# What releases the loads of two granules: landed q transposes of the granule ahead, in place of x transposes two granules before

## The chip, the cores and the metric

The kernel runs on one core of one Trainium2 chip. The metric is the device time of one execution in microseconds (us). Before the change three runs took 208.42, 208.58 and 208.96 us; the median is 208.58 us.

## The reference

The reference is a windowed attention followed by a two-layer feed-forward block. Cut to what matters:

```python
# q, k, v: (4, 8, 768, 64): batch, heads, positions, head size
scores = (q @ k.T) / sqrt(64)
keep = (first 8 keys) | (0 <= i - j < 96)         # global keys and a local window
scores = where(keep, scores - slope[h] * dist, -1e9)
a = softmax(scores)
x = (a @ v), heads side by side                    # (3072, 512)
out = (s * relu(x @ w_in) ** 2 + b) @ w_out        # w_in 512 x 2048, w_out 2048 x 512
```

Inputs and output are float32; the kernel computes in bf16 with sums in float32.

## The kernel before, in words

The 3072 tokens are cut into 12 granules of 256 positions (`NJ`), three for each of the four batches; a granule is two blocks of 128. Each granule goes through the same stations:

- Loads. `load_granule` (lines 110 to 117) issues six DMAs from GpSimd: k and q of the first block, k and q of the second (into the tile `nat`, one of four buffers, `j % 4`), and v of the two blocks (into `vb`). They read float32 from HBM and write bf16; each brings 128 KB. They stand in the trace at lines 116 and 108 (for granules that are loaded piece by piece, at 102 and 108).
- Transposes of k and q. Granules 0 to 3 are transposed on TensorE. From granule 4 on `qk_by_dma` (lines 356 to 363) issues four DMA transposes from SyncE (k, q of the first block, k, q of the second), from `nat` into the tiles `kx` and `qx`. Each is 128 x 512 bf16.
- Scores and attention. `stage_S` (`scores`) multiplies on TensorE at line 441, ScalarE takes the exponential (line 450), VectorE multiplies by a template of the mask (line 457). `stage_A` multiplies by v at line 495, VectorE normalizes into `xn` (lines 465 and 466).
- Transposes of x. `finish_granule` (lines 950 to 957) turns `xn` into `xT`, on TensorE for granules 0 to 3, by two DMA transposes from SyncE (line 599) from granule 4 on.
- The feed-forward block. Its first product is at line 619 (`ps<-xT,w_in_bf`), its second at lines 667 and 819. The stores of the output go out from SyncE at lines 687, 704, 848 and 850.

The order of the work is written out by hand: each engine runs its instructions in program order, and there is no scheduler behind it. The opening (lines 1010 to 1143) is a list of calls; from line 1150 on `step(s, ...)` (lines 959 to 989) does half a granule a time: granule `j = 2 * s // 4`. A step asks for the transposes of granule `j + 2` (if it is the first step of a granule from 4 on), issues the scores of step `s + 1`, then does its two units of attention with pieces of the feed-forward block between them; the second step of a granule calls `finish_granule`, and, for some granules, copies shifted v (`load_voff`, lines 307 to 319, from SyncE). So the scores of granule 5 begin in step 9, of granule 6 in step 11, of granule 7 in step 13, of granule 8 in step 15.

What lets loads start is `hold_loads` (lines 120 to 122): GpSimd copies one element of a tile, and so waits until that tile is written; all loads behind it in GpSimd's queue wait with it. In the kernel before, `finish_granule(j)` puts such a gate on `xT` of granule `j` and, behind it, the loads of granule `j + 4` (`LEAD`), for `j` from 2 to 7. So the loads of granules 6 and 7 are behind the x transposes of granules 2 and 3, which TensorE makes. The loads of granules 4 and 5 are issued before, at lines 1078 to 1082, without a gate. Granule 6's transposes are asked for in step 8 and granule 7's in step 10, both from SyncE, whose queue also carries the stores, the x transposes and the copies of shifted v, in program order.

Of the kernel before, what the change touches and what calls it, by code (L numbers as in the profile page):

```python
# [17 lines left out]
def kernel(  # L18
# [14 lines left out]
    P = nc.NUM_PARTITIONS  # L33
# [9 lines left out]
    HP = H // 2  # L43
    KC = DM // P
    FC = DF // P
    NJ = B * NGR
# [22 lines left out]
    LEAD = 4  # L69
# [5 lines left out]
    NB = S // P  # L75
# [6 lines left out]
    def nat_tile(j):  # L82
        if j not in nat:
            nat[j] = ldp.tile([P, 2, GB, H, D], BF16, name="nat", tag=f"nat{j % 4}", bufs=1)
        return nat[j]
# [3 lines left out]
    def rows_of(src, b, sb):  # L89
        return src[b, :, sb * P : (sb + 1) * P, :].rearrange("h p d -> p h d")  # L90
# [13 lines left out]
    def load_v(j, blocks=range(GB)):  # L104
        b, g = divmod(j, NGR)
        for i in blocks:
            sb = g * GB + i
            nc.gpsimd.dma_start(vbuf[b % 2][:, sb, :, 0:D], rows_of(v, b, sb))  # L108

    def load_granule(j):  # L110
        b, g = divmod(j, NGR)
        t = nat_tile(j)
        for i in range(GB):
            sb = g * GB + i
            for n in range(2):
                nc.gpsimd.dma_start(t[:, n, i, :, :], rows_of(srcs[n], b, sb))  # L116
        load_v(j)


    def hold_loads(ap):  # L120
        g = work.tile([P, 1], BF16, name="gate", tag="gate")
        nc.gpsimd.tensor_copy(g[0:1, :], ap)  # L122
# [156 lines left out]
    def qk_of(b, n):  # L279

        if b not in qk:
            qk[b] = (
                qkp.tile([P, NB, HP, P + (NG + 15) // 16 * 16], BF16, name="kx", tag="kx"),
                qkp.tile([P, NB, HP, P], BF16, name="qx", tag="qx"),
            )
        return qk[b][n][:, :, :, 0:P]
# [9 lines left out]
    def attach(b, lo, hi):  # L296

        kx = qk[b][0]
        nc.vector.tensor_copy(
            kx[:, lo:hi, :, P : P + NG],  # L300
            kx[:, 0, :, 0:NG].unsqueeze(1).to_broadcast((P, hi - lo, HP, NG)),
        )
# [53 lines left out]
    def qk_by_dma(j):  # L356
        b, g = divmod(j, NGR)
        for i in range(GB):
            for n in range(2):
                nc.sync.dma_start_transpose(  # L360
                    qk_of(b, n)[:, g * GB + i],
                    nat[j][:, n, i, :, :].rearrange("p h d -> p (h d)"),
                )
# [12 lines left out]
    def make_koff(j, blocks=range(GB)):  # L376
        b, g = divmod(j, NGR)
        if g == 0 or j >= SHIFT:
            return
        kx, ko = qk[b][0], koff_of(j)  # L380
        i0, n = blocks[0], len(blocks)
        lo = g * GB - 1 + i0
        nc.vector.tensor_copy(ko[:, i0 : i0 + n], kx[:, lo : lo + n, :, 0:P])
        nc.vector.tensor_copy(
            ko[:, i0 : i0 + n, :, 0:NG],
            kx[:, 0, :, 0:NG].unsqueeze(1).to_broadcast((P, n, HP, NG)),
        )
# [83 lines left out]
    def stage_A(u, pool=None):  # L471
        j, hp, b, g = unit(u)
        first = g == 0
        pt = st.pop(u)
        vn = vbuf[b % 2]
        if pool is None:
            av = ps_av.tile([P, GB, 2, VW], F32, name="ps_av", tag="av")
        else:
            av = pool.tile([P, GB, 2, VW], F32, name="ps_av2", tag="psh")
        if j not in xn:  # L480
            xn[j] = xpool.tile([P, GB, DM], BF16, name="xn", tag="xn")
        if first:
            dcol, ocol = ((0, 1), (None, 2)) if j < BIAS_PE else ((1, 2), (None, 0))
        else:
            dcol, ocol = (0, 3), (1, 2)
        for i in range(GB):
            for hi in range(2):
                h = 2 * hp + hi
                terms = [(dcol[i], vn[:, g * GB + i, h, 0 : D + 1])]
                if not first:  # L490
                    terms.append((ocol[i], voff_of(j)[:, i, h, 0 : D + 1]))
                elif i == 1:
                    terms.append((ocol[i], vn[:, 0, h, 0 : D + 1]))
                for n, (c, vv) in enumerate(terms):
                    nc.tensor.matmul(  # L495
                        av[:, i, hi, 0 : D + 1],
                        lhsT=pt[:, hi, c * P : (c + 1) * P],
                        rhs=vv,
                        start=(n == 0),
                        stop=(n == len(terms) - 1),  # L500
                    )
        normalize(
            xn[j][:, :, 2 * hp * D : (2 * hp + 2) * D].rearrange("p i (h d) -> p i h d", d=D), av
        )
# [78 lines left out]
    def x_by_pe(j, evac=(nc.vector.tensor_copy, nc.scalar.copy)):  # L583
        t = xT_tile(j)
        nk = KC // len(evac)
        for e, ev in enumerate(evac):
            ps = ps_h.tile([P, nk, GT], BF16, name="ps_x", tag="psh")
            for kc in range(nk):
                for i in range(GB):
                    c = (e * nk + kc) * P  # L590
                    nc.tensor.transpose(
                        ps[:, kc, i * P : (i + 1) * P], xn[j][:, i, c : c + P], ident_bf[:]
                    )
            ev(t[:, e * nk : (e + 1) * nk, :], ps[:])  # L594

    def x_by_dma(j):
        t = xT_tile(j)
        for i in range(GB):
            nc.sync.dma_start_transpose(t[:, :, i * P : (i + 1) * P], xn[j][:, i, :])

    def g_of(j):

        if j // 2 not in gT:
            gT[j // 2] = gpool.tile([P, FC, 2 * GT], BF16, name="gT", tag="gT")
        return gT[j // 2][:, :, (j % 2) * GT : (j % 2 + 1) * GT]
# [6 lines left out]
    def p1_mm(j, fp):  # L612

        g = g_of(j)
        ps = ps_h.tile([P, 2, GT], F32, name="ps_1", tag="psh")
        for i in range(2):
            fc = 2 * fp + i
            for kc in range(KC):
                nc.tensor.matmul(  # L619
                    ps[:, i, :],  # L620
                    lhsT=w_in_bf[:, kc, fc * P : (fc + 1) * P],
                    rhs=xT[j][:, kc, :],
                    start=(kc == 0),
                    stop=(kc == KC - 1),
                )
        gs = g[:, 2 * fp : 2 * fp + 2, :]

        def relu():
            nc.scalar.activation(gs, ps[:], ACT.Relu)  # L629

        def square():
            nc.vector.tensor_tensor(gs, gs, gs, ALU.mult)  # L632

        return relu, square
# [77 lines left out]
    def flush():  # L712
        while outs:
            outs.pop(0)()
# [222 lines left out]
    def run(cs):  # L937
        for c in cs:
            c()

    def scores(s):
        if s >= NU // 2:
            return []
        _, mms, posts = zip(*[stage_S(u) for u in (2 * s, 2 * s + 1)])
        for part in range(2):
            for mm in mms:
                mm(part)
        return posts[0] + posts[1]

    def finish_granule(j):  # L950
        if j < X_PE:
            x_by_pe(j)
        else:
            x_by_dma(j)
        if 6 <= j + LEAD < NJ:
            hold_loads(xT[j][0:1, 0, GT - 1 : GT])
            load_granule(j + LEAD)

    def step(s, c0, c1, c2, pool=None, pre=()):

        j = 2 * s // HP
        last = (2 * s + 2) % HP == 0
        if not last and j >= 4 and j + 2 < NJ:
            qk_by_dma(j + 2)
        posts = scores(s + 1)
        exps, masks = [c for i, c in enumerate(posts) if i % 2 == 0], posts[1::2]
        run(exps)
        run(pre)
        run(masks)
        run(c0)  # L970
        stage_A(2 * s)
        flush()
        if not last and j + 1 == QK_PE + 1:
            make_koff(j + 1)
        if not last and j % NGR == 0:
            attach(j // NGR, 1, NB)
        run(c1)
        stage_A(2 * s + 1, pool)
        flush()
        n = 2 if j < X_PE else 1  # L980
        run(c2[0:n])
        if last:
            finish_granule(j)
            if SHIFT < j + 2 < NJ:
                load_voff(j + 2)
        run(c2[n:])
        flush()
        if not last and j < SHIFT:
            make_voff(j + 1)
# [130 lines left out]
    p2_mm(1, 1, FC // 2 + 3, FC)  # L1120
    p2_hold(1, 1)
    finish_granule(2)
    s6 = scores(6)
    run(s6)
# [4 lines left out]
    run(scores(7))  # L1129
    run(p1[2][3:5])  # L1130
    qk_by_dma(5)
    r0, q0 = p1_mm(2, 5)
    r0()
    stage_A(14)
# [2 lines left out]
    make_koff(4)  # L1137
    run(p1[2][6:8])
    finish_granule(3)
    run(scores(8))  # L1140
    make_voff(4)
# [110 lines left out]
```

The softmax here doesn't subtract the row's maximum and nothing guards it: scores larger than these inputs give would overflow.

## Time and profile before

| | before |
|---|---|
| median of three runs | 208.58 us |
| lowest and highest run | 208.42 and 208.96 us |
| the profiled execution | 209.15 us |
| its span, first to last instruction | 207.4 us |
| mean granted TensorE clock | 0.998 |
| TensorE busy | 202.1 us |
| VectorE busy | 161.3 us |
| ScalarE busy | 128.5 us |
| GpSimd busy | 68.9 us |
| DMA packets and bytes | 110,836 and 28.17 MB |

The profile is of one execution. Times in it count from the start of its span. PE is TensorE, PEld its weight loads, DVE VectorE, ACT ScalarE, POOL GpSimd and SP SyncE; POOLq and SPq are the queues from which these two issue DMAs. A row of a timeline gives the start, the length, the engine, the line, the operation with the tile that is written and the tile that is read, the number of instructions put together in the row, and, in square brackets, how long the engine had been idle and what ended that. A row of the waits gives who waited, for whom, the total in us, the number of times and the longest. The chain of waits is followed back from the last instruction: at each step to what released it. A DMA's row on its queue is the time in which it is issued; when its data have landed is told apart from that.

### The profile page before, as it was taken

The page shows a single profiled execution, that of the slowest core. Times are in us where ns is not written, and L with a number is a line of the kernel's source. Part 1 is how long each engine was busy: PE and PEld are TensorE (multiplying, and loading weights), DVE is VectorE, ACT ScalarE, POOL GpSimd, SP SyncE. Part 2 cuts the span into 40 slices and gives each one's busy share as a digit, 9 for nine tenths or more (in the row PEclk, how much of TensorE's full clock was granted, in tenths as well). Part 3 has the DMA queues.
Part 4 walks back from the last instruction along what each step waited for, and adds up shares of the span by engine and source line. Part 5 has one row for each costly group of instructions (what it writes and reads, how often), then busy time and mean ns, then how long its engine had stood idle before and what let it go on. Part 6 is the DMA issues. An engine that isn't in the chain of part 4 may idle for free.

```text
span 207.4 us, 5323 instructions
## 1 busy us (share of the span) xinstructions
PE 202.1 (97%) x2191; PEld 160.1 (77%) x2191; DVE 161.3 (78%) x338; ACT 128.5 (62%) x198; POOL 68.9 (33%) x90
## 2 busy tenths in 40 slices
PE   7999999999999999999999999999999999999993
PEld 2678884557867485878888898888888889888883
DVE  7786599977989856799799974699866696737974
ACT  5875669486976548786664595663695764476200
POOL 8985333799365300810900828200000000000000
PEclk9999999999999999999999999999999999999999
DMA  5999999999999999999999999999570300240006
GB/s 164 172 179 202 207 206 177 155 152 129 110 150 120 151 132 218 155 213 212 152 198 153 125 154 178 194 172 126 52 206 0 95 14 0 56 150 0 0 9 196
DMA packets 110836, 28.17 MB, mean 136 GB/s; under 512 B 97852, under 2 KB 109308, under 8 KB 110812
## 3 DMA queue, kind: packets, MB, share of 16 engines
q0 software_dynamic: 76000, 13.11, 90.1%
q1 hardware_dynamic: 33612, 14.13, 41.7%
q10 hardware_dynamic: 1200, 0.59, 1.1%
q8 instruction: 17, 0.28, 0.6%
q14 instruction: 7, 0.06, 0.1%
HBM read 27.26 MB, written 6.29 MB: 162 GB/s over the span
## 4 chain that ended last, share of the span: by engine, by line
PE 65%; DMA 23%; POOL 9%; issue 1%; DVE 0%; POOLq 0%
PE ps L619 29%; PE ps L819 24%; DMA nat<-in_q_dram 12%; DMA w_in_bf<-in_moe_w_in_dram 6%; PE ps L667 5%; DMA qx<-nat 4%; PE ps_s L441 4%; PE ps_av L495 3%; POOL vb L108 3%; POOL nat L102 3%; POOL w_in_bf L140 2%; POOL nat L116 1%; PE ps_last L819 0%; DVE o_last L828 0%; POOL rel L173 0%
## 5 line engine op out<-in xcount | busy, mean ns | idle before, releaser
L619 PE MATMUL ps<-xT,w_in_bf 128*128 128x256 bf16 x768 | 90.3, 273 | 0.0
L629 ACT ACTIVATE gT<-ps 128x512 bf16<-128x512 f32 x96 | 55.8, 599 | 46.8 <-PE ps L619 46.6
L619 PEld LDWEIGHTS <-w_in_bf 128*128 128x128 bf16 x768 | 73.0, 98 | 9.4 <-DVE xT L594 0.2
L450 ACT ACTIVATE pt<-ps_s 128x1024 bf16<-128x1024 f32 (+1 forms) x44 | 39.3, 946 | 3.3 <-PE ps_s L441 3.3
L667 PE MATMUL ps<-w_out_bf,gT 128*128 128x512 bf16 x128 | 29.7, 380 | 0.0
L457 DVE TENSOR_TENSOR pt<-pt,tmpl 128x1024 bf16<-128x1024 bf16 (+1 forms) x40 | 24.6, 645 | 3.8 <-ACT pt L450 3.7
L819 PEld LDWEIGHTS <-gsum 128*128 128x128 bf16 x256 | 24.1, 98 | 3.7 <-DVE gsum L782 0.5
L108 POOL DMA_DIRECT2D vb<-in_v_dram x24 | 21.4, 906 | 6.9 <-DMA w_out_bf<-in_moe_w_out_dram 3.4
L793 DVE TENSOR_TENSOR gT<-gT 128x1024 bf16<-128x1024 bf16 x20 | 13.7, 686 | 11.7 <-ACT gT L629 11.7
L667 PEld LDWEIGHTS <-gT 128*128 128x128 bf16 x128 | 11.7, 98 | 13.0
L466 DVE TENSOR_TENSOR xn<-ps_av,rc 128x256 bf16<-128x256 f32 x48 | 20.4, 425 | 1.7
L819 PEld LDWEIGHTS <-gT 128*128 128x128 bf16 x200 | 18.6, 98 | 2.3
L465 DVE RECIPROCAL rc<-ps_av 128x4 f32<-128x4 f32 x48 | 8.6, 179 | 12.3 <-PE ps_av L495 10.4
L116 POOL DMA_DIRECT2D nat<-in_k_dram x16 | 14.2, 885 | 9.2 <-DMA nat<-in_k_dram 5.1
L495 PEld LDWEIGHTS <-pt 128*128 128x128 bf16 x320 | 14.4, 97 | 2.7 <-DVE xn L466 0.7
L632 DVE TENSOR_TENSOR gT<-gT 128x512 bf16<-128x512 bf16 x32 | 13.0, 422 | 3.5 <-ACT gT L629 3.3
L495 PE MATMUL ps_av<-vb,pt 128*128 128x65 bf16 x208 | 15.5, 193 | 0.0
L819 PE MATMUL ps<-w_out_bf,gsum 128*128 128x256 bf16 x128 | 15.3, 273 | 0.0
L116 POOL DMA_DIRECT2D nat<-in_q_dram x16 | 14.2, 888 | 2.9 <-DMA w_in_bf<-in_moe_w_in_dram 1.9
L819 PE MATMUL ps<-wsub,gsum 128*128 128x256 bf16 x128 | 15.1, 273 | 0.0
L819 PE MATMUL ps<-w_out_bf,gT 128*128 128x256 bf16 x120 | 13.9, 273 | 0.0
L122 POOL COPY gate<-xT 1x1 bf16<-1x1 bf16 x6 | 1.1, 176 | 35.9 <-DMA xT<-xn 35.9
(112 smaller groups left out, 228.5 us busy)
## 6 DMA issues: line engine op xcount, KB each, us to landing
out_dram<-o_q SPq DMA_DIRECT2D x15, 256.0 KB, 2.6
vb<-in_v_dram POOLq DMA_DIRECT2D x24, 128.0 KB, 8.3
nat<-in_k_dram POOLq DMA_DIRECT2D x22, 128.0 KB, 7.7
nat<-in_q_dram POOLq DMA_DIRECT2D x22, 128.0 KB, 7.6
w_out_bf<-in_moe_w_out_dram POOLq DMA_DIRECT2D x4, 512.0 KB, 16.2
w_in_bf<-in_moe_w_in_dram POOLq DMA_DIRECT2D x4, 256.0 KB, 7.4
w_in_bf<-in_moe_w_in_dram POOLq DMA_DIRECT2D x2, 512.0 KB, 11.3
out_dram<-o_sb SPq DMA_DIRECT2D x4, 256.0 KB, 6.3
```

The source lines that it names most:

```text
L108: nc.gpsimd.dma_start(vbuf[b % 2][:, sb, :, 0:D], rows_of(v, b, sb))
L116: nc.gpsimd.dma_start(t[:, n, i, :, :], rows_of(srcs[n], b, sb))
L450: nc.scalar.activation(pt[:, :, 0:ncol], ps[:, :, 0:ncol], ACT.Exp, scale=QSCALE)
L457: nc.vector.tensor_tensor(pv, pv, m.rearrange("p h a c -> p h (a c)"), ALU.mult)
L466: nc.vector.tensor_tensor(dst, av[:, :, :, 0:D], rc[:].to_broadcast((P, 2, 2, D)), ALU.mult)
L495: nc.tensor.matmul(av[:, i, hi, 0 : D + 1], lhsT=pt[:, hi, c * P : (c + 1) * P], rhs=vv, start=(n == 0), stop=(n == len(terms) - 1),)
L619: nc.tensor.matmul(ps[:, i, :], lhsT=w_in_bf[:, kc, fc * P : (fc + 1) * P], rhs=xT[j][:, kc, :], start=(kc == 0), stop=(kc == KC - 1),)
L629: nc.scalar.activation(gs, ps[:], ACT.Relu)
L632: nc.vector.tensor_tensor(gs, gs, gs, ALU.mult)
L667: nc.tensor.matmul(po[:], lhsT=g_of(j)[:, fc, tb * P : (tb + 1) * P], rhs=w_out_bf[:, fc, :], start=(fc == 0), stop=(fc == FC - 1),)
L793: outs.append(lambda: nc.vector.tensor_tensor(gs, gs, gs, ALU.mult))
L819: nc.tensor.matmul(ps[:, tb, cs], lhsT=stat[:, fc, tb * P : (tb + 1) * P], rhs=mov[:, fc, cs], start=(fc == 0), stop=(fc == NH - 1),)
```

## The change

The gate in `finish_granule` now serves only granules from 8 on (`j` from 4). The loads of granule 6 get a gate of their own in the opening: they stand behind the call that issues the transposes of granule 5, and wait until the last of these four (q of the second block) has landed. The loads of granule 7 likewise stand behind the transposes of granule 6 in step 8, and wait for the last of those. The same loads, the same transposes and the same number of gate copies are issued, each engine's instructions keep their order, and nothing else in the program differs.

```diff
 def finish_granule(j):
     if j < X_PE:
         x_by_pe(j)
     else:
         x_by_dma(j)
-    if 6 <= j + LEAD < NJ:
+    if 8 <= j + LEAD < NJ:
         hold_loads(xT[j][0:1, 0, GT - 1 : GT])
         load_granule(j + LEAD)
...
 def step(s, c0, c1, c2, pool=None, pre=()):
...
         if not last and j >= 4 and j + 2 < NJ:
             qk_by_dma(j + 2)
+            if j == 4:
+                hold_loads(qk_of(2, 1)[0:1, 1, HP - 1, P - 1 : P])
+                load_granule(7)
...
     run(p1[2][3:5])
     qk_by_dma(5)
+    hold_loads(qk_of(1, 1)[0:1, NB - 1, HP - 1, P - 1 : P])
+    load_granule(6)
     r0, q0 = p1_mm(2, 5)
```

## The prediction

> **What bounds the kernel now.** I read the page's busy shares first, then what TensorE waited for, then the chain that ended last around those waits, then the queues of GpSimd and SyncE in order of time. The page says that TensorE is the bound:
>
> ```profile
> PE 202.1 (97%) x2191; PEld 160.1 (77%) x2191; DVE 161.3 (78%) x338; ACT 128.5 (62%) x198; POOL 68.9 (33%) x90
> ```
>
> TensorE works 202.1 of 207.4 us. No change of DMA order can give back more than its idle time, so the list of its waits is the ceiling of any gain:
>
> ```profile
> PE ps_w L161 <- DVE idle L151: 1.2, 1, 1.2
> PE ps_s L441 <- DMA qx<-nat: 0.5, 1, 0.5
> ```
>
> The first stands at the start, before any load of this change. Only the second, once, 0.5 us, can be touched. The chain of waits shows how it comes about (start, length, what):
>
> ```profile
> 48.56 11.61 DMA nat<-in_q_dram
> 60.17 0.02 issue
> 60.19 8.86 DMA qx<-nat
> 69.06 0.04 issue
> 69.10 0.57 PE ps_s L441 x14
> ```
>
> The last q block of granule 5 takes 11.61 us to load, its transpose by DMA another 8.86, and TensorE takes up the scores of granule 5 (in step 9) at 69.10. From there the chain runs on TensorE to the end, so the wait is on the path, and a later one would be as well. The GpSimd queue shows what ran beside that transpose (start, us, line, what, idle before):
>
> ```profile
> 51.16 0.18 POOL L122 COPY gate<-xT 1x1 bf16<-1x1 bf16 x1
> 51.28 0.88 POOL L116 DMA_DIRECT2D nat<-in_k_dram  x1
> ...
> 61.62 0.18 POOL L122 COPY gate<-xT 1x1 bf16<-1x1 bf16 x1
> 61.74 0.87 POOL L116 DMA_DIRECT2D nat<-in_k_dram  x1
> ...
> 83.29 0.18 POOL L122 COPY gate<-xT 1x1 bf16<-1x1 bf16 x1 [11.86 <-DMA xT<-xn]
> ```
>
> The 12 loads of granules 6 and 7 are issued between 51.28 and 71.4 us and occupy the DMA engines to about 80 us. The question is when each is needed. In TensorE's timeline the scores are entered at 68.4 (granule 5; 0.5 us of waiting follows), 81.7 (granule 6), 94.1 (granule 7) and 108.7 (granule 8).
>
> [...]in the DMA view of 65.5 to 66 us
>
> ```profile
> q0 software_dynamic: 207, 0.03, 80.0%
> q1 hardware_dynamic: 204, 0.05, 78.9%
> ```
>
> GpSimd's loads (q0) and SyncE's transposes (q1) share one to one, some 410 packets a us each; 1,194 packets a us of q0 alone went between 59.2 and 60.2 us, and 1,102 of q1 alone between 82.6 and 83.6. A load is 1,024 packets, a transpose 512, so a transpose takes some 1.25 us beside loads and 0.5 us alone. [...]all these loads stay in one queue in program order; the trace shows all 68 k, q and v loads there. [...]here a load with nothing else queued still took 4.1 us to land (granule 10's first).
>
> **The change, part by part.**
>
> 1. Removed: two gates (0.18 us each on GpSimd) on the x transposes of granules 2 and 3. Added: two like them, on the last q transposes of granules 5 and 6. GpSimd is idle between its loads, and behind a waiting gate stand only later loads. Cost of the copies themselves: nothing. SyncE's own order does not change, only the time at which its transposes find their data.
>
> 2. Loads of granule 6 leave the stretch from 51 us. Queue q0 is in order, so granule 5's k, q and v loads, already ahead, land when they do now (60.17 for the last q, about 61.5 for v). After that q0 is empty, and granule 5's transposes have the engines alone: four of them at 0.5 us, the last issued at 60.19 to 61.73. The lightly loaded transposes of granule 9 landed 2.5 and 3.4 us after issue; with a remainder of v in the way I take 4.1: landed at 64.3 (bounds 63 and 66) instead of 69.06. TensorE wants it at 68.4, so the 0.5 us stall goes: **-0.5 us**, and all needs below move up by 0.5.
>
> 3. Each later granule now goes through a link "gate, 4 k/q loads, 4 transposes". Its price stands in the trace: granule 10's gate opens at 114.52, its first load is issued at 115.12, SyncE issues the last transpose at 124.05 to 125.27 and that lands at 127.77 (read from the landing events). So gate to the end of issue on SyncE is 10.75 us and gate to landed 13.25. Upper bound: granule 8's loads took 10.3 us from gate to the last q landing (83.29 to 93.6), and the page's median landing of a loaded transpose is near 6, so 16.5 us. Lower: 12.
>  - Granule 6: gate 64.3, landed 77.5, needed at 81.2: slack 3.7 us.
>  - Granule 7: gate 77.5, landed 90.8, needed at 93.6: slack 2.8 us. Two links in series, so an error of 1 us in each takes 2 of it.
>
> 4. What stands behind these transposes on SyncE. Its queue is in order, so x transposes and stores wait for granule 6's and 7's loads too. After granule 6's four (issued until 64.3 + 10.75 = 75.05) come two stores at some 0.53, then the x transposes of granule 4: free at 76.1. Today they start at 76.17 because their data (DVE's xn) end at 76.13. No cost. After granule 7's four (until 77.5 + 10.75 = 88.3) come one store and three early stores, four at about 0.5, then the x transposes of granule 5: about 90.3, where today it is
>
> ```profile
> 84.49 0.53 SPq L687 DMA_DIRECT2D out_dram<-o_sb  x1
> 85.11 4.64 SPq L704 DMA_DIRECT2D out_dram<-o_early  x3
> 89.92 2.96 SPq L599 DMA_TRANSPOSE xT<-xn  x2
> ```
>
>  These landed at 97.6 (the gate of granule 9 opens at 97.71), and TensorE uses them at 98.35: 0.65 us of slack is all there is. With 0.4 us lost on SyncE, the need 0.5 us earlier, and 1 MB of stores now issued in 2 us ahead of them rather than spread over 5, I take 0.9 to 1 us less slack: a new wait of **+0.3 us** at the first phase-1 matmuls of granule 5 (step 13). Bounds: 0 if the stores drain as before; 2 if both links come out 1 us longer.
>
> 5. Loads of granule 8: their gate (x of granule 4) should still open by 83, but GpSimd is issuing granule 7's loads until 77.5 + 0.6 + 5.3 = 83.4. So they start at about 84, as now (83.87). Granule 7's v, last in its group of loads, lands near 89; the copies that read it (`load_voff`, on SyncE at 93) don't wait. From granule 8 on the order is that of today; the scores of granule 8 are needed at 108.2 and its transposes start on SyncE near 95.9 against 95.59 today. Nothing.
>
> Sum: -0.5 + 0.3 = -0.2 us. The profiled execution took 209.15 us (span 207.4, some 1.75 around it) and gives 208.95; the median of the runs shown is 208.58, 0.57 below that, so I forecast 208.58 - 0.2 = **208.4 us**.
>
> **Rivals.**
>
> - *Clean gain.* The x transposes of granule 5 land in time as well, and the whole 0.5 us stays: 208.1. For it: stores may drain faster with q0 briefly empty; against: 0.65 us of slack today is little. More than 0.5 is not there to be had.
> - *The series of links is too long (the other side).* Mechanism: the loads of granules 6 and 7 can no longer run ahead; each link must end before the next begins, and SyncE, blocked in front of granule 7's transposes, holds back the x transposes of granule 5. It decides from a link of about 13.6 us upward (slack gone on x of granule 5) and 14.6 (scores of granule 7, whose slack is 2.8 over two links). At 15 us a link, SyncE is done with granule 7 at 64.3 + 15 + 12.5 = 91.8, the x transposes start near 93.8, 3.9 after today's: stall 3.9 - 0.65 + 0.5 = 3.7 if all of it shows, some 2 if the later, lighter queue q0 gives part back. Net +1.5: 210.1. For it: the medians in loaded stretches (7.4 us for a load, 6 to 7 for a transpose); against: granule 10's link, a like one, took 13.25. At the upper 16.5 the time would reach some 212.
> - *The transposes of granule 5 don't land earlier.* If what delays them isn't q0's share, the stall stays and the chain begins at 69.1: granule 6 landed at 82.3, granule 7 at 95.6, x of granule 5 later by 5: some 211. Against it: the one-to-one sharing above.
>
> **How the numbers follow.** A measurement of this kernel can tell about 0.3%, 0.63 us, from no change. Forecast (a part given back) 0.45, within that bound; clean gain 0.2, of which 0.06 is read as faster by over 0.3% through scatter; links too long 0.3, slower; no earlier transposes 0.05, slower. Of the forecast's chance, 0.02 goes to slower. So faster 0.06, same 0.57, slower 0.37. The range runs from the clean gain less the scatter of the runs (0.2) to the 15 us link: 207.9 to 210.1; above it lies about 0.17. The cases of the likely sign alone have 207.9 to 208.9.
>
> **What would show it.** The wait of L441 on qx at 69 us gone and the landing of that transpose near 64 (step 2); the gates of granules 6 and 7 at about 64.3 and 77.5 (step 3); the scores of granules 6 and 7 without a wait; the x transposes of granule 5 issued near 90.3 and a short TensorE wait for them at 98 (step 4); granule 8's loads from 84 (step 5). I am wrong if a link takes over 14 us, if TensorE waits at the scores of granule 7, or if the first gate opens after 66.

## The result, and the profile after

| | before | after |
|---|---|---|
| median of four runs | 208.50 us | 214.16 us |
| lowest and highest run | 208.34 and 208.96 | 212.82 and 214.91 |
| ratio, 95% interval | | 1.026 (1.0206 to 1.0315) |
| the profiled execution | 209.15 us | 213.95 us |
| its span | 207.4 us | 212.2 us |
| TensorE busy | 202.1 us | 203.5 us |
| mean granted clock | 0.998 | 0.991 |

The change makes the kernel 2.6% slower; the forecast was 208.4 us, no measurable difference, with a range that ended at 210.1. Here and below a ratio leaves out executions more than 1.5% above the fastest of the same kernel, while a median keeps them.

TensorE's longest waits in the changed kernel (who waited for whom, total, times, longest):

```profile
PE ps L619 <- DMA xT<-xn: 3.0, 1, 3.0
PE ps_w L161 <- DVE idle L151: 1.2, 1, 1.2
PE ps_s L441 <- ACT qx L331: 0.3, 1, 0.3
PE ps_s L441 <- DMA qx<-nat: 0.2, 1, 0.2
```

The first row is new: 3 us on x of a granule. The wait of before (L441 on qx at 69 us) is gone; the L441 row on qx that is here now stands elsewhere, as TensorE's timeline shows:

```profile
93.75 0.23 PE L441 MATMUL ps_s<-qx,kx 64*128 64x128 bf16 x2
94.23 0.57 PE L441 MATMUL ps_s<-qx,kx 64*128 64x128 bf16 x14 [0.24 <-DMA qx<-nat]
94.73 3.67 PE L819 MATMUL ps<-w_out_bf,gT 128*128 128x256 bf16 x32
98.23 0.34 PE L495 MATMUL ps_av<-vb,pt 128*128 128x65 bf16 x6
101.62 2.83 PE L619 MATMUL ps<-xT,w_in_bf 128*128 128x256 bf16 x16 [3.05 <-DMA xT<-xn]
104.25 0.54 PE L495 MATMUL ps_av<-vb,pt 128*128 128x65 bf16 x6
104.60 2.53 PE L619 MATMUL ps<-xT,w_in_bf 128*128 128x256 bf16 x16
107.06 0.62 PE L441 MATMUL ps_s<-qx,kx 64*128 64x128 bf16 x16
107.61 1.92 PE L619 MATMUL ps<-xT,w_in_bf 128*128 128x256 bf16 x16
```

At 94 the scores of granule 7 wait for granule 7's transposes; at 101.62 the first product of granule 5 (step 13) has waited 3.05 us for granule 5's x. Then see the lengths: 16 matmuls of 128x256 take 2.83 and 2.53 us, and 1.92 from 107.61 on. The windows name the reason (stretch, length, busy of PE, PEld, DVE, ACT and POOL with their instructions, then the granted TensorE clock as a share of full speed, the DMA share, GB/s):

```profile
98.50:101.60 3.10, 0.08 (x3) 0.00 (x0) 1.41 (x4) 0.00 (x0) 0.00 (x0) 1.00 1.47 143
101.60:104.46 2.86, 2.84 (x20) 2.22 (x21) 0.00 (x0) 0.60 (x1) 2.34 (x4) 0.65 1.30 215
104.46:107.10 2.64, 2.64 (x24) 1.97 (x23) 1.20 (x3) 1.19 (x2) 2.64 (x4) 0.73 1.83 232
107.10:110.00 2.90, 2.90 (x45) 2.58 (x45) 2.21 (x4) 2.84 (x5) 0.45 (x1) 1.00 1.99 215
```

The 0.65 and 0.73 are means of stretches in which the clock stood at half for a part: from 102.46 to 105.87, for 3.41 us, the granted clock is 0.50. That costs half of it, 1.7 us, and comes on top of the wait.

GpSimd's queue of the changed kernel, with its gates (the sixth row is that of granule 8):

```profile
64.31 0.60 POOL L122 COPY gate<-qx 1x1 bf16<-1x1 bf16 x1 [13.42 <-DMA qx<-nat]
64.85 0.88 POOL L116 DMA_DIRECT2D nat<-in_k_dram  x1
...
77.13 0.18 POOL L122 COPY gate<-qx 1x1 bf16<-1x1 bf16 x1 [7.00 <-DMA qx<-nat]
77.63 0.88 POOL L116 DMA_DIRECT2D nat<-in_k_dram  x1 [0.32 <-PE ps_s L441]
...
81.10 1.79 POOL L108 DMA_DIRECT2D vb<-in_v_dram  x2
82.84 0.18 POOL L122 COPY gate<-xT 1x1 bf16<-1x1 bf16 x1
82.96 0.88 POOL L116 DMA_DIRECT2D nat<-in_k_dram  x1
...
101.70 0.18 POOL L122 COPY gate<-xT 1x1 bf16<-1x1 bf16 x1 [13.48 <-DMA xT<-xn]
```

The new gates open at 64.31 and 77.13, and granule 8's loads follow granule 7's without a pause. SyncE's queue of the changed kernel, from granule 7's last transpose on:

```profile
87.13 1.26 SPq L360 DMA_TRANSPOSE qx<-nat  x1
88.49 0.53 SPq L687 DMA_DIRECT2D out_dram<-o_sb  x1
89.11 1.46 SPq L704 DMA_DIRECT2D out_dram<-o_early  x3
90.68 2.66 SPq L599 DMA_TRANSPOSE xT<-xn  x2
```

The x transposes are issued 0.76 us later than before (89.92) and land at 101.6 instead of 97.6. What the DMA engines did meanwhile, 94.5 to 96.5 us in the changed kernel (packets, MB, share):

```profile
q1 hardware_dynamic: 336, 0.61, 92.0%
q0 software_dynamic: 334, 0.04, 32.3%
```

Granule 8's loads (q0) and SyncE's queue (q1, here nearly all packets of the four stores, 2 KB each) moved packet for packet here, 334 to 336. In the kernel before, the packets of granule 7's transposes had all moved by 87 us, and behind them q1 had only stores and x to carry. Earlier in the changed kernel the queues did not even share: from 87 to 88 us, with two of granule 7's transposes issued by 87.04 that landed at 91.65 and 93.01, they moved

```profile
q0 software_dynamic: 1166, 0.15, 273.0%
q1 hardware_dynamic: 5, 0.00, 0.7%
```

(The share adds up the times of all packets, and passes 100% where they overlap.)

The sum, change against before in the two profiled executions: the opening, which the change doesn't touch, was late by 0.3 us (scores of granule 5 entered at 68.68 against 68.36); -0.7 by the end of the wait at 69; +0.4 at the scores of granule 7; +3.2 at x; +1.6 by the slow clock (the last product starts 4.84 us later than before, the one at 101.62 3.27 later). 0.3 - 0.7 + 0.4 + 3.2 + 1.6 = 4.8, and the spans differ by 4.8.

### The profile page after: what moved, and what is told of

It reads as the page before. It is cut to its first block, busy times and chain, and to the rows that moved or that the text cites. A ratio compares the mean times of both kernels' runs of the same rounds, so it can differ in the third digit from the quotient of the medians.

```text
span 212.2 us, 5313 instructions
## 1 busy us (share of the span) xinstructions
PE 203.5 (96%) x2183; PEld 161.3 (76%) x2191; DVE 160.7 (76%) x338; ACT 128.4 (61%) x198; POOL 70.1 (33%) x90
## 4 chain that ended last, share of the span: by engine, by line
PE 90%; DMA 6%; DVE 1%; ACT 1%; issue 0%; SPq 0%
PE ps L619 40%; PE ps L819 21%; PE ps L667 13%; PE ps_s L441 5%; PE ps_av L495 5%; DMA xT<-xn 4%; DMA first<-in_k_dram 2%; PE ps_t L351 1%; PE ps_s L517 1%; PE ps_t L327 1%; PE ps_x L591 1%; PE ps_s L532 1%; PE ps_s L416 1%; PE ps_av L558 1%; PE ps_t L341 0%; PE ps_last L819 0%
## 5 line engine op out<-in xcount | busy, mean ns | idle before, releaser
L619 PE MATMUL ps<-xT,w_in_bf 128*128 128x256 bf16 x768 | 91.9, 275 | 3.1 <-DMA xT<-xn 3.0
L667 PE MATMUL ps<-w_out_bf,gT 128*128 128x512 bf16 x120 | 28.7, 380 | 0.5 <-issue 0.2
L795 ACT ACTIVATE gT<-gT 128x1024 bf16<-128x1024 bf16 x12 | 12.7, 1057 | 0.4
```

The lines of the kernel that those rows point to most:

```text
L619: nc.tensor.matmul(ps[:, i, :], lhsT=w_in_bf[:, kc, fc * P : (fc + 1) * P], rhs=xT[j][:, kc, :], start=(kc == 0), stop=(kc == KC - 1),)
L667: nc.tensor.matmul(po[:], lhsT=g_of(j)[:, fc, tb * P : (tb + 1) * P], rhs=w_out_bf[:, fc, :], start=(fc == 0), stop=(fc == FC - 1),)
```

## The experiments

Theory A: what is late is a transpose that has the next granule's loads beside it. Where the next loads follow at once, the link (gate, loads, transposes) becomes long, and with it all that stands behind it in SyncE's queue. Rival B: two links in series are too long by themselves. Rival C: it is the four stores, pressed together ahead of x. Theory D came with the second set: what is lost is DMA time while a gate is shut. "Gate 6" is the gate of granule 6's loads, and so on; the time given for a gate is that at which it opens in the profiled execution. Times of waits and landings are of profiled executions as well. The diffs are against the changed kernel, and cut where "..." stands.

**One gate alone.** First, gate 6 alone:

```diff
-        if 8 <= j + LEAD < NJ:
+        if 7 <= j + LEAD < NJ:
...
-            if j == 4:
-                hold_loads(qk_of(2, 1)[0:1, 1, HP - 1, P - 1 : P])
-                load_granule(7)
```

> Only the loads of granule 6 wait for the transposes of granule 5; those of granule 7 follow them at once, behind the x transposes of granule 3, long done. Theory A (what costs is that the loads of the next granule follow at once and share the DMA engines one to one with the transposes, x transposes and stores that stand in SyncE's queue): the trouble moves one granule ahead; granule 6's transposes land near 81.4 instead of 77.1, x of granule 4 near 85 where TensorE wants it at 83.5: a wait of some 1.5 to 2 us and perhaps a slow clock behind it, 209.5 to 212. Rival B (two gated links in series are what is too long): one link has room enough, no wait, the 0.75 us of the old wait are gained: 207.8.

212.0 us, ratio 1.0144 (1.0106 to 1.0182), as A had it. Gate 6 opens at 64.45 and the gate ahead of granule 7's loads at 70.5, as soon as GpSimd has issued those of granule 6; x of granule 4 comes late. TensorE's timeline in this kernel:

```profile
81.81 1.24 PE L667 MATMUL ps<-w_out_bf,gT 128*128 128x512 bf16 x5
85.49 3.19 PE L619 MATMUL ps<-xT,w_in_bf 128*128 128x256 bf16 x16 [2.44 <-DMA xT<-xn]
```

A wait of 2.44 us, and a slow clock (3.19 us for 16 matmuls, a granted clock of 0.52 from 86.0 to 89.5), one granule ahead of the changed kernel's. Rival B, which gave one link room enough, fails here. Then gate 7 alone:

```diff
-        if 8 <= j + LEAD < NJ:
+        if j + LEAD == 6 or 8 <= j + LEAD < NJ:
...
-    hold_loads(qk_of(1, 1)[0:1, NB - 1, HP - 1, P - 1 : P])
-    load_granule(6)
```

> Only the loads of granule 7 wait for the transposes of granule 6; those of granule 6 start at 51 us as before the change. Theory A: gate 7 opens at about 79, granule 7's transposes land near 96 and x of granule 5 near 103.5, because granule 8's loads again follow at once: waits of 1.5 to 2 us at the scores of granule 7 and 3 us at x, and the slow clock: 213 to 216. Rival B: a single link in series, some 2 us later than in the changed kernel's plan but with nothing ahead of it: at most 2 us of wait, 210 or below.

209.41 us, ratio 1.0037 (1.0019 to 1.0054). A's number is wrong (B's bound, 210 or below, holds): I had gate 7 open at 79, and it opened at 73.98, because granule 6's transposes, with no loads of granule 7 beside them, landed 5 us sooner than I had them. That is A's own mechanism, which I had not applied to this link. In the profiled execution, 208.78 us, TensorE waits for no q, k or x at all. But 5 of the 20 executions took 212.1 to 213.0 us at a mean clock of 0.990 to 0.992, as slow as the changed kernel or nearly so, and the ratio leaves them out; what TensorE waited for in them no profile shows. The loss has become rarer and isn't gone. Gate 6 is the costlier of the two.

**What lies beside the transposes.** The loads of granule 8 are held as well:

```diff
-        if 8 <= j + LEAD < NJ:
+        if 9 <= j + LEAD < NJ:
...
                 load_granule(7)
+            if j == 5:
+                hold_loads(qk_of(2, 1)[0:1, 3, HP - 1, P - 1 : P])
+                load_granule(8)
```

> As the changed kernel, and the loads of granule 8 also wait, for the last transpose of granule 7, so that no loads run beside granule 7's transposes. Theory A: these land near 91 instead of 94.2, x of granule 5 lands near 95 to 96 instead of 101.6, no wait of TensorE at either; granule 8 is in time (needed near 108): 207.8. Rival B: three links in series are worse than two: the waits stay and one at the scores of granule 8 is added, 215 or more. Rival C (the four stores pressed together ahead of x of granule 5 are the cause): x lands near 98.5, a wait of 0.3 us or so remains, 208.5.

212.25 us, ratio 1.0139 (1.0095 to 1.0182). Half of A came true: granule 7's transposes land at 90.6 instead of 94.2, x of granule 5 at 97.8 instead of 101.6, and there is no wait at either. But granule 8 is not in time, as A had assumed. TensorE's timeline of this kernel:

```profile
108.24 0.23 PE L441 MATMUL ps_s<-qx,kx 64*128 64x128 bf16 x2
110.96 0.57 PE L441 MATMUL ps_s<-qx,kx 64*128 64x128 bf16 x14 [2.49 <-DMA qx<-nat]
```

The lateness has moved on to the scores of granule 8, whose transposes have granule 9's loads (gate at 97.88) beside them. Then the loads of granule 8 are left out altogether, so that its attention is computed from what lies in the buffers and its part of the output isn't the reference's:

```diff
             hold_loads(xT[j][0:1, 0, GT - 1 : GT])
-            load_granule(j + LEAD)
+            if j + LEAD == 8:
+                nat[8] = nat[4]
+            else:
+                load_granule(j + LEAD)
```

> As the changed kernel, but the six loads of granule 8 are left out (its attention is computed from what lies in the buffers, so its part of the output is not the reference's). Gates and gaps stay. Theory A (next granule's loads beside the transposes make them late): granule 7's transposes land near 91, x of granule 5 near 95, TensorE waits for neither and keeps its clock: 207.5 to 208. Rival B (the two links in series are too long by themselves): the wait of 3 us at x and the slow clock stay: 212 to 214.

208.52 us, ratio 0.9999 (0.9984 to 1.0014). Both gates stand as in the changed kernel (64.63 and 77.57), the four stores are ahead of x as there, x of granule 5 lands at 97.4, and the longest waits are

```profile
PE ps_w L161 <- DVE idle L151: 1.2, 1, 1.2
PE ps_s L441 <- ACT qx L331: 0.3, 1, 0.3
PE ps L619 <- DMA xT<-xn: 0.3, 1, 0.3
```

The loss is gone with six loads. Rival B falls: the two links fit. C falls as the whole cause: the stores alone don't make x late. (A was nearly right on the waits; it had x land 2.4 us too early, and its time, 207.5 to 208, was 0.5 us too low at least.)

**The stores.** The four stores that stand ahead of x of granule 5 on SyncE are issued behind it and behind the copies of shifted v (the fifth store of steps 10 and 11 stood there already):

```diff
-        nc.sync.dma_start(out[t0 : t0 + P, :], o_sb[:])
+        send(out[t0 : t0 + P, :], o_sb[:])     # cut: a list keeps it back from step 10 on
...
                 load_voff(j + 2)
+            if j == 5:
+                later[0] = False
+                while held:
+                    held.pop(0)()
```

> As the changed kernel, but the five stores of steps 10 and 11 are issued from SyncE behind the x transposes of granule 5 and the copies of shifted v, so that nothing but granule 7's transposes is ahead of x. Theory A and rival C: granule 7's transposes land near 94.2 as in the changed kernel (wait of 0.4 us), x near 97, no wait: 208.2 to 208.5. If the loads beside it alone decide and the stores don't matter, x lands near 100 and a wait of 2 us stays: 210 to 212.

211.53 us, ratio 1.012 (1.0083 to 1.0156); A and C both had 208.2 to 208.5. x lands at 97.4, near what they said, and TensorE doesn't wait for it. But the scores of granule 7 wait 1.9 us here (0.24 in the changed kernel), in an execution of 210.59 us. To move the stores is worth about half the loss, and they are not the cause of the rest. Set beside the kernel without granule 8's loads this says more: taking away either, the loads or the stores, brings x from 101.6 back to 97.4. Its lateness needs both.

**The slow clock.** Matmuls that nobody reads fill the wait:

```diff
+    def fill(n):
+        ps = ps_h.tile([P, CH], F32, name="ps_f", tag="psh")
+        for _ in range(n):
+            nc.tensor.matmul(ps[:], lhsT=ones_bf[:], rhs=w_in_bf[:, 0, 0:CH], start=True, stop=True)
...
-            [u1(o, 0)],
+            [lambda: fill(26), u1(o, 0)] if pr == 2 else [u1(o, 0)],
```

> As the changed kernel, and TensorE does 26 matmuls of 128x256 whose product nobody reads (some 2.8 us) just ahead of the first product of granule 5 in step 13, where the changed kernel waits 3 us for x. If the half clock behind that wait (3.41 us of it, from 102.5 to 105.9) comes from TensorE's standing idle, the clock stays full there, x lands when it did, and about 1.7 us are gained: 212.3 to 212.8. If the clock falls for another reason, or falls anyway, or the filler only adds to the work: 214 or more.

212.80 us, ratio 1.0195 (1.0162 to 1.0228), against 214.16 and 1.026 of the changed kernel: 1.4 us less, though the two intervals overlap a little. The clock is the clearer sign. x lands at 101.6 as before, the wait behind the filler is 0.7 us, and the clock stays at 1.0; the mean clock of the six executions is 0.997 to 1.000, where three of the changed kernel's four have 0.984 to 0.991. (Its fourth, at 1.000, took 212.82 us.) So what brought the slow clock here is TensorE's standing idle, though not in every execution.

**Using the gap in the loads.** The DMA view of the changed kernel from 61 to 66 us has no q0 row at all:

```profile
## 3 DMA queue, kind: packets, MB, share of 16 engines
q1 hardware_dynamic: 1143, 0.27, 71.3%
q8 instruction: 1, 0.02, 1.5%
```

No load moves for 5 us; in the kernel before the loads run without such a gap until 82.1. The v loads of granules 6 and 7 are put there:

```diff
     qk_by_dma(5)
+    load_v(6)
+    load_v(7)
     hold_loads(qk_of(1, 1)[0:1, NB - 1, HP - 1, P - 1 : P])
-    load_granule(6)
+    load_granule(6, False)                     # k and q alone; granule 7 likewise
```

> As the changed kernel, but the four v loads of granules 6 and 7 are issued ahead of gate 6, at 51 us, and only the k and q loads stand behind gates 6 and 7. The queue of loads, empty from 61.0 to 66.2 and from 75.2 to 79.6 us in the changed kernel, then has 3.4 us of work in the first gap and 3.4 us less behind the gates. Theory D (what is lost is the run-ahead: DMA time that goes unused while a gate is shut comes back as lateness later, wherever SyncE's queue is fullest): granule 8's loads end some 3 us sooner, x of granule 5 lands near 99, a wait below 1 us, often with no slow clock: 209 to 211.5. Rival B (the series of two gated links itself): the gates open when they did or up to 2 us later, so no gain: 214 or more.

213.36 us, ratio 1.0219 (1.0191 to 1.0247). Theory D missed. With v beside granule 5's transposes gate 6 opens at 68.1 instead of 64.3, and TensorE waits 3.3 us for x of granule 4. Filling the gap with the v loads made the transposes that the next link waits for 3.8 us later. Next, gate 6 is opened earlier, on the landed loads of granule 5:

```diff
-    hold_loads(qk_of(1, 1)[0:1, NB - 1, HP - 1, P - 1 : P])
+    hold_loads(nat[5][0:1, 1, 1, H - 1, D - 1 : D])
```

> As the changed kernel, but gate 6 waits only until the last k or q load of granule 5 has landed (near 60), not its transposes, so the first gap in the loads nearly closes; gate 7 is unchanged. Theory D: gate 7 opens near 75 instead of 77.1, the wait at x of granule 5 falls below 1.5 us, the wait of 0.5 us on granule 5's transposes may come back: 210 to 212. Rival B: as the changed kernel less at most 2 us, 212 to 214.

209.05 us, ratio 1.0021 (1.0004 to 1.0038), better than either theory. Gate 6 opens at 59.95, gate 7 at 73.97, as in the kernel with gate 7 alone; the times are alike too. The profiled execution is one of the late ones, 212.02 us (it and one of 345.46 us, at a clock of 0.561, whose cause isn't known, are not in the ratio). TensorE waits for x of granule 5 in it:

```profile
101.28 1.92 PE L619 MATMUL ps<-xT,w_in_bf 128*128 128x256 bf16 x16 [2.47 <-DMA xT<-xn]
```

So the changed kernel's wait can still come with the gates 4.4 and 3.2 us earlier. The 16 matmuls behind it take 1.92 us, and those that follow are as fast: here the clock did not fall.

**Where the two gates may stand.** With gate 6 as in the changed kernel, gate 7 on the landed loads of granule 6:

```diff
-                hold_loads(qk_of(2, 1)[0:1, 1, HP - 1, P - 1 : P])
+                hold_loads(nat[6][0:1, 1, 1, H - 1, D - 1 : D])
```

> As the changed kernel with gate 6 untouched, but gate 7 waits only until the last q load of granule 6 has landed (near 74) and not for its transpose (77.1). Theory A with a deadline (a link with the next loads right behind it takes about 17 us from its gate; what counts is by when gate 7 opens): as in the two kernels in which gate 7 opened at 74.0, the wait at x of granule 5 goes or nearly so; the last transposes of granule 6 now have loads beside them, so x of granule 4 lands later, a wait of 0 to 1.5 us there: 208.5 to 211. If the opening of gate 6 at 64.3 decides by itself, wherever gate 7 stands: 213 to 214.5.

213.44 us, ratio 1.0233 (1.0211 to 1.0254). Gate 7 opens at 73.96, but the wait only changes place, to x of granule 4:

```profile
PE ps L619 <- DMA xT<-xn: 3.3, 1, 3.3
```

So gate 7's time alone is not the deadline. With gate 6 at 64.3 to 64.5 no place for gate 7 was found that is right: at 70.5 and 74 x of granule 4 is late, at 77.1 x of granule 5. Both earlier, gate 6 on the landed loads of granule 5 again and gate 7 on the first block of granule 6's transposed q:

```diff
-                hold_loads(qk_of(2, 1)[0:1, 1, HP - 1, P - 1 : P])
+                hold_loads(qk_of(2, 1)[0:1, 0, HP - 1, P - 1 : P])
```

> Gate 6 on the landed loads of granule 5 (near 60), gate 7 on the first block of granule 6's transposed q (72 to 73). Theory A with a deadline: gate 7 is 1 to 2 us earlier than the 74.0 at which most runs had no wait, so fewer runs with one: 208.2 to 208.8.

209.53 us, ratio 1.0059 (1.0039 to 1.0079): missed. Gate 7 opens at 72.46, and a wait of 0.8 us at x of granule 4 is there. Last, both on landed loads, gate 6 on those of granule 5 and gate 7 on those of granule 6:

> Both gates wait for landed loads only, of granule 5 (near 60) and of granule 6 (near 69). The loads then run nearly without a gap, as before the change. Theory A: the same as before the change within 0.3%, 208.2 to 208.9; the wait of 0.5 us on granule 5's transposes may be gone or not.

208.44 us, ratio 0.9995 (0.9987 to 1.0003). The gates open at 58.92 and 68.52, the loads run with gaps of 2.6 and 1.4 us, and no wait for q, k or x is left:

```profile
PE ps_w L161 <- DVE idle L151: 1.2, 1, 1.2
PE ps_s L441 <- ACT qx L331: 0.2, 1, 0.2
```

It is the best of all versions, none of its 13 executions took over 208.81 us, and it is not measurably better than the kernel before.

**The 0.5 us of the kernel before.** The same kernel, profiled once more:

> The kernel before, unchanged, profiled a second time, for the 0.5 us that the forecast counted as a gain. If the wait of TensorE on granule 5's transposes belongs to every execution, it stands in this profile too, at some 0.5 us near 69 us, and the kernel with both gates on landed loads, which has no such wait, should have been 0.5 us faster than it was. If it comes and goes with the moment at which loads land, it is absent or of another size here, and the gain was never there in the median.

208.59 us, ratio 1.0 (0.9991 to 1.001); this execution took 208.32 us. Its waits are

```profile
PE ps_w L161 <- DVE idle L151: 1.2, 1, 1.2
PE ps_t L327 <- DVE nat L260: 0.4, 1, 0.4
PE ps L667 <- issue: 0.2, 1, 0.2
```

No wait for granule 5's q: its last transpose landed at 67.6, 0.6 us ahead of TensorE, where in the first profile it landed at 69.06. The wait that the forecast set out to gain comes in some executions and not in others.

## Why the prediction was wrong, point by point

- *What bounds the kernel.* Right: TensorE is the bound, and the waits that came are on the path. But the wait of 0.5 us was taken from one profile for a property of the kernel; in the second it is absent.
- *Step 2, granule 5's transposes land at 64.3.* Right: gate 6 opens at 64.31. The -0.5 us is in the changed kernel's trace, but not in the median of the kernels without that wait (208.44 and 208.52 against 208.5 to 208.8 of the kernel before).
- *Step 3, the price of a link.* Here it failed. The 13.25 us of granule 10's link were used twice. Granule 6's link took 77.1 - 64.3 = 12.8 us, granule 7's 94.2 - 77.1 = 17.1, above the upper bound of 16.5. What was mis-sized is the last part, from the end of SyncE's issue to the landing: 2.5 us in the model link (125.27 to 127.77), 5.8 for granule 7 (88.39 to 94.2). The model link had no loads behind it: granule 11's gate opened at 124.9, when granule 10's transposes were nearly issued. (Nor was its first load alone, as the forecast says: from 115.1 to 116.5 us 747 packets of SyncE's queue moved.) Behind granule 7's loads those of granule 8 follow at 82.96. I had used the sharing of the DMA engines (207 packets to 204) for granule 5 and then left it out for granule 7. And one to one, read from half a microsecond, is not the whole of it. From 87 to 88 us the loads moved 1,166 packets in the changed kernel, nearly the 1,194 of the kernel before from 59.2 to 60.2, where no other packet moved, and SyncE's queue, with transposes issued and not landed, moved 5.
- *Step 4, SyncE's queue.* The issue of x was right: 90.3 forecast, 90.68 measured. Its landing was mis-sized: 0.4 us later by the forecast, 4.0 measured (101.6 against 97.6). The x transposes stood behind granule 7's transposes (landed at 94.2) and four stores, and all three had granule 8's loads beside them. That is the +0.3 us that measured 3.2. Without the six loads, or with the stores out of the way, x lands at 97.4: it is the two together.
- *Step 5, "granule 8's loads start as now: nothing".* They start about as now (82.96 against 83.87), and cost all the same, by what is now beside them. A transfer that doesn't move has to be looked at again when its neighbour does.
- *A term that was missing.* The half clock behind a wait: 1.7 us in the changed kernel (half of the 3.41 us at a granted clock of 0.50), 1.4 us by the filler. What lets it come behind one wait and not behind another isn't shown: behind a wait of 2.44 us (gate 6 alone) the 16 matmuls took 3.19 us, behind one of 2.47 us (gate 6 on landed loads) 1.92.
- *The rivals.* "The series of links is too long" named the right place (x of granule 5), the right side and, at its upper end, a time of 212; the half clock was not in it. Its mechanism did not come: SyncE was hardly held up (x issued at 90.68), and the series is refuted by the kernel without granule 8's loads, and by the slow kernel with gate 6 alone. Its threshold of 13.6 us a link also disagrees with the forecast's own sum, in which x is late at 13.25. I gave the slower cases together 0.37, and times above the range 0.17.

Why gate 6 is the one that decides is not settled. In the profiled executions with gate 6 at 64.3 to 64.6, all loads kept and no filler, a wait of 1.9 to 3.3 us came in every arrangement of the later gates and stores, at x of 4, the scores of 7, x of 5 or the scores of 8. With gate 6 at 60 or earlier the ratio is 1.006 at most, but single executions still lose 3.3 to 4.4 us: five of twenty with gate 7 alone, and the profiled one with gate 6 on landed loads. That it is DMA time lost in the gaps, theory D, does not fit the traces as a plain sum: with both gates earlier no load moved for 2.6 and for 5.1 us, 7.7 in all, at a ratio of 1.0059; with gate 6 alone it was one gap of 5.6 us, at 1.0144.

## What to carry to other kernels

A load that ran ahead of its need looked like interference with the transfer beside it (a wait of 0.5 us), but to hold it back turned it here into interference with the next one, on a shorter deadline (a wait of 3.05 us). Of the gates tried, only those that wait for landed loads alone, for both granules, cost nothing. The price taken from a later stage, 13.25 us, did not hold where other transfers followed: granule 7's link took 17.1. Look at what is issued behind the model step before using it. And a wait of half a microsecond in a single profile should be seen in a second one before a change is built on it.

## What the runs showed of the hardware

- A wait of TensorE cost up to 1.7 us beyond itself. In the changed kernel the wait of 3.05 us is followed by a granted clock of 0.50 for 3.41 us. Behind waits of 2.44 us (gate 6 alone), 3.27 us (v loads first) and 3.3 us (gate 6 as changed, gate 7 on landed loads) the next 16 matmuls of 128x256 took 3.19, 3.19 and 2.50 us, where 16 took 1.91 at a granted clock of 1.00 (changed kernel, 89.8 and 91.7 us); behind one of 2.49 us (gate 8 too) 27 took 4.79 us, where 32 took 3.67 at 1.00 (changed kernel, 94.7 us). The mean clock of these five executions is 0.989 to 0.992. Behind a wait of 1.9 us (stores behind x) 32 took 3.67 us, and behind one of 2.47 us (gate 6 on landed loads) 16 took 1.92, at mean clocks of 0.997 and 1.0. So the length of a wait alone does not tell; what else decides wasn't shown.
- Two queues that both had work moved packet for packet in some stretches of the changed kernel: from 94.5 to 96.5 us 336 packets of SyncE's queue, 298 of them store packets of 2 KB, went beside 334 load packets of 128 bytes, and from 98.5 to 99.0 us 202 of SyncE's queue, transposes of 256 bytes a packet, beside 204 of loads. So the loads moved 167 packets a us beside these stores and 408 beside these transposes; in the kernel before from 59.2 to 60.2 us, where no packet of SyncE's queue moved, it was 1,194. In other stretches the counts were far apart. In the changed kernel from 87 to 88 us it was 1,166 to 5 beside transposes that were issued and not landed, and in the kernel before from 92 to 93 us 1,138 to 12, beside stores that had all been issued by 89.75 and still moved packets after 94. What held SyncE's queue back there wasn't tried.
- Both queues nearly stopped for half a microsecond in some stretches, with transfers issued and not landed in both: from 100.0 to 100.5 us in the changed kernel 11 packets of each moved, where 204 and 202 did from 98.5 to 99.0, and from 63.0 to 63.5 us in the kernel before 13 of the loads and 14 of SyncE's queue. What made them stop wasn't tried.
